# DeltaNet and a PReLU feed-forward on one core: outputs accumulated in PSUM and turned on VectorE instead of TensorE

## The chip, the core and the metric

One core of a Trainium2 chip runs the whole program. The metric is the device time of one execution in microseconds (us). Five engines work side by side, each through its own queue in order: TensorE (PE, with its weight loads as PEld), VectorE (DVE), ScalarE (ACT), GpSimd (POOL) and SyncE (SP, which issues nearly all DMAs). Work between engines is ordered by semaphores.

## What is computed

A delta-rule attention is followed by a feed-forward layer; the attention's output, with heads laid side by side, is the feed-forward's input.

```python
# q, k, v: (4 batches, 8 heads, 768, 48); beta: (4, 8, 768)
k_n = k / (norm(k) + 1e-6)
for t in range(768):
    y[t]  = q[t] @ state                     # the state before this token
    v_old = k_n[t] @ state
    state = state + beta[t] * outer(k_n[t], v[t] - v_old)
x = y as (3072 tokens, 384)
h = x @ w_in                                 # 384 x 2048
out = (max(h, 0) + alpha * min(h, 0)) @ w_out   # 2048 x 384
```

All of it is float32.

## The kernel before

**Chunks and steps.** The 768 tokens are cut into 12 chunks of 64. A step n is one chunk for two of the four batches: 24 steps, `steps[n] = (c, bp)`, so an even and the following odd step make up one chunk c (n = 2c and 2c + 1). A chunk's 256 token rows are the unit of the feed-forward.

**One step of attention.** In the order of the data: `through_state` (L799) multiplies keys with the state and with the turned queries; three VectorE subtractions (L809) make the right-hand side r and L521 masks the query-key products a_t. `solve` (L824) multiplies r with the inverse of the chunk's triangular matrix, and L828 weighs the result to u. `outputs` (L837) multiplies a_t with u, `next_state` (L853) keys with u, and L861 subtracts that from the state. `query` (L784) multiplies the queries with the state before the step; ScalarE copies the result from PSUM to y (L788), and L843 on VectorE adds the product of `outputs` to it. `to_ffn` (L876) turns y on TensorE, three 128x128 transposes against the identity into a PSUM bank, and L878 on ScalarE copies the turned block into xt, the feed-forward's input for the chunk.

**Preparing later steps.** `grams` (L501) multiplies keys with keys eight steps ahead; L507 weighs the result in two VectorE pieces, `keep` (L554) moves one block. Every four steps, `eliminate` inverts the small triangular blocks on VectorE in many short pieces (L593, L599) with 32x32-block transposes (L566). `between` (L733) builds the off-diagonal blocks, which ScalarE copies out (L745). `turn_q` (L466) turns a step's queries by one VectorE transpose, `load_q` fetches them (SP).

**The feed-forward.** `ffn_in` (L966) multiplies xt with w_in, 512 columns to a PSUM bank; L976 on ScalarE takes the negative part and L978 on VectorE adds it with its slope. `ffn_out_fast` (L1031) multiplies with w_out by seven products instead of eight; the operand sums are L920. From chunk 8 on `ffn_in_fast` (L1189 to L1237) and `ffn_out_faster` (L1283) do the same with fewer TensorE products and with more work on ScalarE, GpSimd and VectorE; L1151 makes sums of the chunk's xt beforehand.

**The order.** The order on every engine is written out by the program. From step 6 (JOINED) on, each step has two bursts of attention products on TensorE, and the feed-forward, a generator of equal parts, fills the stretches between: `burst_a` (outputs and next_state of step n - 1, through_state of step n), a filled stretch, `turn_round` (to_ffn of step n - 1, then the turn of keys, of queries n + 2, the weights and load_q n + 3), a second stretch, `burst_b` (solve n, grams n + 9, query n + 1, between), a third stretch. FILL and FILLS say how many parts each stretch takes: 12, 10, 12 in even and 12, 18, 12 in odd steps. A chunk's feed-forward has 76 parts, which is what two steps take. `weave` interleaves the pieces of other engines by their share of a stretch.

**PSUM.** From step 8 (NARROW) on there are two double banks for the attention (p_pair) and four single banks for the feed-forward (p_ffn, p_more). `ps_big` hands out the double banks in turn. Different engines reading the same bank are ordered one behind the other.

Of the kernel before, what the change touches and what calls it, by code (L numbers as in the profile page):

```python
# [25 lines left out]
FP32 = mybir.dt.float32  # L26
# [18 lines left out]
def kernel(  # L45
# [31 lines left out]
    def ps_big():  # L77

        big.append(big.pop(0))
        return big[-1]  # L80
# [24 lines left out]
    def half(i):  # L105
        return slice(64 * i, 64 * i + 64)

    def dims(i):
        return slice(64 * i, 64 * i + D)
# [375 lines left out]
    def now(pieces):  # L485
        for x in pieces:
            x()
# [7 lines left out]
    def grams(n, p=None):  # L495

        if n >= N:
            return []
        p = region(p, G * C, g=G)
        for g, a, t in quarters():  # L500
            nc.tensor.matmul(  # L501
                p[half(t), a, g], k_t[n][dims(a), g, half(t)], k_t[n][dims(a), g, half(t)]
            )

        def weighted(dst, cols):
            w = stats[n][1][:, 0:2, :, None].to_broadcast([128, 2, G, HB])
            nc.vector.tensor_tensor(  # L507
                out=dst.rearrange("p (a g) i -> p a g i", a=2), in0=p[:, :, :, cols], in1=w,
                op=ALU.mult,
            )  # L510

        return [
            lambda: weighted(gather(n), slice(0, HB)),
            lambda: weighted(right[n % EARLY][:, 1:], slice(HB, C)),
            lambda: keep(n),
        ]
# [136 lines left out]
    def quad(i):  # L653
        return slice(HB * i, HB * i + HB)
# [123 lines left out]
    def query(n, p=None):  # L778
        if n >= N:
            return []  # L780
        bp = steps[n][1]
        p = region(p, G * D, g=G)
        for g, a, t in quarters():
            nc.tensor.matmul(  # L784
                p[half(t), a, g], q_t[n][dims(a), t, g], state[bp][dims(a), t, g]
            )
        ys[n] = work.tile([128, H, D], FP32, name="y")
        return [lambda: nc.scalar.copy(by_parity(ys[n]), p)]  # L788

# [31 lines left out]
    def solve(n, p=None):  # L821
        p = region(p, G * D, g=G)
        for g, a, t in quarters():
            nc.tensor.matmul(  # L824
                p[half(t ^ a), a, g], inv[n % NE][half(t), a * G + g], rhs_[n][half(t), a, g]
            )
        us[n] = work.tile([128, 2, G, D], FP32, name="u")
        return [lambda: nc.vector.tensor_tensor(  # L828
            out=us[n], in0=p,
            in1=stats[n][1][:, 0:3:2, :, None].to_broadcast([128, 2, G, D]), op=ALU.mult,  # L830
        )]

    def outputs(n, p=None):
        c, bp = steps[n]
        p = region(p, G * D, g=G)
        for g, a, t in quarters():
            nc.tensor.matmul(  # L837
                p[half(t), a, g], a_t[n][half(t ^ a), a * G + g], us[n][half(t ^ a), a, g]
            )
        if c == 0:  # L840
            ys[n] = work.tile([128, H, D], FP32, name="y")
            return [lambda: nc.scalar.copy(by_parity(ys[n]), p)]
        return [lambda: nc.vector.tensor_tensor(  # L843
            out=by_parity(ys[n]), in0=by_parity(ys[n]), in1=p, op=ALU.add
        )]

    def next_state(n, p=None):
        c, bp = steps[n]
        pieces, wide = [], n < 2 * NJ
        if c < NCH - 1:  # L850
            p = region(p, G * D, g=G)
            for g, a, t in quarters():
                nc.tensor.matmul(  # L853
                    p[half(a) if wide else dims(a), t, g], k_late[n % NKL][half(t ^ a), 2 * g + a, 0 : C if wide else D],
                    us[n][half(t ^ a), a, g],
                )


            def less(rows):
                x = state[bp][rows]  # L860
                nc.vector.tensor_tensor(out=x, in0=x, in1=p[rows], op=ALU.subtract)  # L861

            if wide:
                pieces = [lambda: less(slice(0, 2 * C))]
            else:
                pieces = [lambda: less(dims(0)), lambda: less(dims(1))]
        return pieces

    def to_ffn(n, p=None):
        c, bp = steps[n]  # L870
# [500 lines left out]

    WY, JOINED = G * D, NJ + 2

    def burst_a(n):

        soon, later = [], []
        b = ps_big()
        if n > JOINED:
            soon += outputs(n - 1, b[:, :, 0:WY])
            soon += next_state(n - 1, b[:, :, WY : 2 * WY])  # L1380
            later.append(lambda: load_late(n + 1))
        if n < N:
            p = ps_big()
            y = ps_big()[:, :, 0:WY] if n < NARROW else None
            soon += through_state(n, p[:, :, 0 : G * (D + C)], y)
            if n < JOINED + 2:
                soon += between_1(n + 1, b[:, :, 2 * WY : 2 * WY + G * HB])
            if n == JOINED:
                soon += grams(n + EARLY, big[-1][:, :, WY : WY + G * C])
                later.append(lambda: squares(n + EARLY + 1))  # L1390
            later.append(lambda: load_v(n + 3))
        now(soon)
        return later

    def burst_b(n):

        b, x = ps_big(), ps_big()
        soon = solve(n, b[:, :, 0:WY])
        gram = grams(n + EARLY + 1, x[:, :, 0 : G * C])
        asked = query(n + 1, x[:, :, G * C : G * C + WY]) if n + 1 >= NARROW else []  # L1400
        wanted = [(n + 1, True, b[:, :, WY : WY + G * HB])]
        if n > JOINED:
            wanted.append((n + 2, False, b[:, :, 2 * WY : 2 * WY + G * HB]))
        soon += between(*wanted)
        if n >= LATE:
            now(soon[:1])
            return soon[1:] + asked
        now(soon + asked + gram[:2])
        return gram[2:] + [lambda: squares(n + EARLY + 2), lambda: load_early(n + EARLY + 3)]

    def turn_round(n):

        if n > JOINED:
            to_ffn(n - 1)
        if n == JOINED:
            flips(n + EARLY + 1, N)
            load_keys(steps[TURNED_K][0])
        later = []
        if TURNED_K <= n + EARLY + 1 < N:
            later.append(lambda: turn_k(n + EARLY + 1))  # L1420
        if n + 2 < N:
            later.append(lambda: turn_q(n + 2))
        later += weigh(n + EARLY + 1)
        return later + [lambda: load_q(n + 3)]
# [427 lines left out]
    TURNS = [(3, 3, 4), (3, 3, 4), (4, 4, 4), (0, 5, 6)]  # L1852
    FILL = {JOINED: (8, 12, 12), JOINED + 1: (10, 12, 10), JOINED + 2: (8, 10, 12)}
    FILLS = [(12, 10, 12), (12, 18, 12)]
    put_off = []
    for n in range(JOINED, N):
        if n == NARROW:
            banks(2, 2)
        fill, share = FILL.get(n, FILLS[n % 2]), PIECES_OF.get(n, TURNS[n % NJ])
        extra = [[], [], []]  # L1860
        if n == JOINED:
            place(n + 1, (0,))
            extra[1] = [(weight_sums(1, 0, 3), 3)]
            extra[2] = [(weight_sums(0, 3, 4), 1)]
        elif n == JOINED + 1:
            extra[0] = [(weight_sums(1, 3, 4), 1, 0.6), (placing(n + 1, (1, 2, 3)), PLACING)]

        later = burst_a(n)
        stretch(fill[0], blocks, share[0], later, *extra[0], *put_off)
        put_off = []  # L1870
        later = turn_round(n)
        if n == JOINED:
            extra[1].append((placing(n + 1, (1, 2, 3)), PLACING))
        stretch(fill[1], blocks, share[1], later, *extra[1], soon=0.2)
        m, ends = (n + 6) // NJ, n % NJ == 2
        if ends and n > JOINED:
            for _ in blocks:
                assert False
            place(n + 2, (0,))
        later = burst_b(n) + [lambda: scale_v(n + 1)]  # L1880
        if n == JOINED:
            stretch(fill[2], blocks, share[2], later, *extra[2])
            for _ in blocks:
                assert False
            place(n + 2, (0,))
            place(n + 3, (0,))
            blocks = eliminate(m)
        else:
            if ends:
                blocks = eliminate(m) if m < N // NJ else iter(())  # L1890
            after = [(placing(n + 2, (1, 2, 3)), PLACING)]
            if n % NJ != 1:
                after.append((placing(n + 3, (0,)), 1))
            if n >= LATE:
                put_off, after = after, []
            stretch(
                fill[2], blocks, share[2], later, *after, *extra[2], soon=0.1 if n >= LATE else 0.5
            )
# [34 lines left out]
```

## Time and profile before

| | |
|---|---|
| median of 3 runs | 647.7 us (647.32 to 648.19) |
| the profiled execution | 647.16 us |
| its span in the trace | 645.4 us |
| TensorE busy | 630.1 us (98%) |
| VectorE busy | 502.9 us (78%) |
| ScalarE busy | 253.0 us (39%) |
| GpSimd busy | 94.0 us (15%) |
| granted TensorE clock | 0.999 of full speed |

The span is the time from the first to the last instruction of the core in the trace; the execution lies 1.8 us around it. Matmuls are pipelined, so a busy TensorE may still not be at its peak; the chain of work that ended last and the waits tell whether it was held up. In the views, a line such as L876 is a line of the kernel before; tiles carry the program's names.

### The profile page before, as it was taken

Reading aid. Unit: us, or ns where it says so; the run is one execution under the profiler, and the core shown is the slowest. Engines: PE = TensorE matmul, PEld = TensorE weight load, DVE = VectorE, ACT = ScalarE, POOL = GpSimd, SP = SyncE. Lnnn points to the kernel's source line nnn. Section 1 sums busy time; section 2 is a strip of 40 time slices with the busy share of each in tenths; the row PEclk is TensorE's granted clock in tenths of the full one; section 3 lists DMA queues with packets and bytes.
Section 4 is the critical chain, followed back from the end, with each engine's and each line's share of the span. In section 5 each row is a group of like instructions: output and inputs, shape, how many; then the busy total and the mean of one; then the engine's idle time right before and its main releaser. Section 6 shows DMA issues by size and latency. Waiting matters only on the chain.

```text
span 645.4 us, 21564 instructions
## 1 busy us (share of the span) xinstructions
PE 630.1 (98%) x9199; PEld 556.2 (86%) x9199; DVE 502.9 (78%) x1206; ACT 253.0 (39%) x599; POOL 94.0 (15%) x204
## 2 busy tenths in 40 slices
PE   5999999999999999999999999999999999999997
PEld 4678888557778988988988988988999999999997
DVE  3986988977999879768979869769879569477383
ACT  5978565344453342243242243133145054041240
POOL 6001211010000000001000000000044053062360
PEclk9999999999999999999999999999999999999999
DMA  8967725211353243242242122122121220100000
GB/s 122 296 136 170 232 60 153 62 38 35 52 79 51 39 65 51 38 67 48 39 76 39 25 46 32 26 47 30 32 51 20 42 36 2 39 1 3 26 0 25
DMA packets 145968, 39.26 MB, mean 61 GB/s; under 512 B 139040, under 2 KB 142256, under 8 KB 145872
## 3 DMA queue, kind: packets, MB, share of 16 engines
q1 hardware_dynamic: 144000, 37.40, 28.4%
q8 instruction: 72, 1.18, 0.8%
q10 hardware_dynamic: 1872, 0.49, 0.4%
q14 instruction: 24, 0.20, 0.1%
HBM read 33.14 MB, written 4.72 MB: 59 GB/s over the span
## 4 chain that ended last, share of the span: by engine, by line
PE 77%; DVE 13%; ACT 5%; issue 2%; DMA 2%; SPq 1%; POOL 1%; DVEq 0%; POOLq 0%; ACTq 0%
PE p_ffn L966 12%; PE p_more L1283 8%; PE p_more L1031 7%; PE p_ffn L1031 7%; PE p_more L966 7%; PE p_ffn L1009 5%; PE p_more L1199 5%; PE p_ffn L1189 3%; PE p_ffn L1283 3%; PE p_ffn L1194 2%; DVE block L599 2%; PE p_pair L799 2%; PE p_pair L837 2%; PE p_pair L824 2%; PE p_pair L733 2%
## 5 line engine op out<-in xcount | busy, mean ns | idle before, releaser
L966 PE MATMUL p_ffn<-xt,w_in 128*128 128x256 f32 x528 | 123.1, 384 | 1.8 <-DVE act L978 1.8
L966 PEld LDWEIGHTS p_ffn<-xt,w_in 128*128 128x128 f32 x528 | 97.5, 190 | 16.0 <-ACT wgt L718 1.6
L966 PE MATMUL p_more<-xt,w_in 128*128 128x256 f32 x240 | 54.8, 381 | 0.0
L599 DVE TENSOR_TENSOR block<-block,prod 128x30 f32<-128x30 f32 (+9 forms) x150 | 49.8, 332 | 5.2
L1223 POOL TENSOR_TENSOR k_t<-k_t 128x128 f32<-128x128 f32 (+1 forms) x48 | 29.6, 616 | 163.7 <-ACT k_t L1218 161.2
L878 ACT COPY xt<-p_pair 128x384 f32<-128x384 f32 x22 | 10.4, 479 | 107.5 <-PE p_pair L876 107.3
L966 PEld LDWEIGHTS p_more<-xt,w_in 128*128 128x128 f32 x240 | 45.0, 190 | 6.3
L593 DVE TENSOR_TENSOR prod<-block 128x30 f32<-128x30 f32 (+9 forms) x150 | 48.8, 325 | 1.5
L418 POOL TENSOR_TENSOR beta_t<-beta_t,rec 128x8 f32<-128x8 f32 x24 | 5.9, 245 | 280.0 <-DVE rec L412 270.4
L976 ACT ACTIVATE act<-p_ffn 128x512 f32<-128x512 f32 x36 | 21.4, 593 | 53.1 <-PE p_ffn L966 53.0
L978 DVE SCALAR_TENSOR_TENSOR act<-act,al_t,p_ffn 128x256 f32<-128x256 f32 x72 | 30.9, 471 | 8.7 <-ACT act L976 8.6
L1223 POOL TENSOR_TENSOR block<-block 128x128 f32<-128x128 f32 (+1 forms) x48 | 28.0, 583 | 15.8 <-ACT block L1218 13.3
L1189 PE MATMUL p_ffn<-xt,w_in 128*128 128x256 f32 x96 | 28.7, 380 | 0.0
L1031 PE MATMUL p_ffn<-w_out,act 128*128 128x192 f32 x160 | 27.9, 330 | 0.0
L507 DVE TENSOR_TENSOR same<-p_pair,wgt 128x256 f32<-128x256 f32 x24 | 10.1, 422 | 22.3 <-ACT y L788 17.0
L745 ACT COPY inv<-p_pair 32x256 f32<-32x256 f32 x40 | 14.5, 362 | 33.1 <-DVE u L828 32.3
L976 ACT ACTIVATE act<-p_more 128x512 f32<-128x512 f32 x20 | 11.9, 595 | 37.2 <-PE p_more L966 37.2
L1031 PEld LDWEIGHTS p_ffn<-w_out,act 128*128 128x128 f32 x160 | 25.9, 190 | 0.4
L809 DVE TENSOR_TENSOR r<-v_raw,p_pair 64x192 f32<-64x192 f32 (+1 forms) x66 | 23.3, 352 | 2.3 <-PE p_pair L799 1.2
L828 DVE TENSOR_TENSOR u<-p_pair,wgt 128x384 f32<-128x384 f32 x24 | 13.2, 554 | 14.4 <-PE p_pair L733 13.6
L1031 PE MATMUL p_more<-w_out,act 128*128 128x192 f32 x128 | 22.2, 328 | 0.0
L1009 PE MATMUL p_ffn<-w_out,act 128*128 128x384 f32 x64 | 21.7, 490 | 0.2 <-ACT w_out L262 0.2
(252 smaller groups left out, 1489.5 us busy)
## 6 DMA issues: line engine op xcount, KB each, us to landing
w_out<-in_moe_w_in_dram SPq DMA_DIRECT2D x10, 512.0 KB, 5.6
v_raw<-in_v_dram SPq DMA_DIRECT2D x48, 96.0 KB, 2.8
kl<-in_k_dram SPq DMA_DIRECT2D x96, 48.0 KB, 2.5
out_dram<-o_sb SPq DMA_DIRECT2D x90, 48.0 KB, 1.6
space_out<-in_moe_w_out_dram SPq DMA_DIRECT2D x11, 384.0 KB, 4.3
ke_last<-in_k_dram SPq DMA_DIRECT2D x25, 96.0 KB, 3.1
qp<-in_q_dram SPq DMA_DIRECT2D x64, 32.0 KB, 2.2
w_out<-in_moe_w_out_dram SPq DMA_DIRECT2D x5, 384.0 KB, 4.5
```

Of the source, the lines that this page charges most:

```text
L593: nc.vector.tensor_tensor(out=prod, in0=r[:, 0:j, j : j + 1].to_broadcast([128, j, n]), in1=r[:, j : j + 1, j + 1 : HB].to_broadcast([128, ...
L599: nc.vector.tensor_tensor(out=r[:, 0:j, j + 1 : HB], in0=r[:, 0:j, j + 1 : HB], in1=prod, op=ALU.add)
L809: nc.vector.tensor_tensor(out=r[to, a], in0=v_in[to, a], in1=p[own, a, :, 0:D], op=ALU.subtract)
L966: nc.tensor.matmul(p_h[:, i], w_in[:, t, (f + i) * 128 : (f + i + 1) * 128], xt[:, t], start=(t == 0), stop=(t == KT - 1),)
L976: nc.scalar.activation(g, p_h, ACT.Relu, scale=-1.0)
L978: nc.vector.scalar_tensor_tensor(out=g[:, i], in0=g[:, i], scalar=al_t[:, f + i : f + i + 1], in1=p_h[:, i], op0=ALU.mult, op1=ALU.add,)
L1009: nc.tensor.matmul(p_o[u], gs[f // 2][:, f % 2, u * 128 : (u + 1) * 128], w_out[:, f], start=(f == 0), stop=(f == FT - 1),)
L1031: nc.tensor.matmul(p, x(i), w(i), start=(i == 0), stop=(i == FP - 1))
L1189: nc.tensor.matmul(p[:, f * 256 : f * 256 + 256], w(2, f), xt[:, 2], start=True, stop=False)
L1199: nc.tensor.matmul(q[:, j], a, b, start=True, stop=True)
L1223: nc.gpsimd.tensor_tensor(out=dst, in0=a, in1=b, op=ALU.add)
L1283: nc.tensor.matmul(p, x(i), w(i), start=(i == 0), stop=(i == FP - 1))
```

## The change

From step 8 on, y is no longer put together on VectorE. The query product and the outputs product of a step go into the same PSUM region: `query` starts the accumulation and `outputs`, half a step later, adds to it. For this the query of step n moves from `burst_b` of step n - 1 to `burst_b` of step n, ahead of the solve, and its bank (`asked_in`) is kept for `burst_a` of step n + 1. ScalarE then copies the finished sum to y, where it copied the query product before.

The turn of y for steps 8 to 22 moves off TensorE. `turn_y` is one VectorE transpose of 32x32 blocks, issued in the burst right behind the state's subtraction. `rows_y` is sixteen ScalarE copies of 32 partitions by 96 elements that put the blocks into xt. In odd steps (the first half of a chunk) eight of them go to the second and eight to the third stretch; in even steps (the second half, which completes the chunk) all sixteen go to the first stretch, from 0.4 of it on. Step 23 keeps `to_ffn`.

`turn_q` of step n + 2 moves from `turn_round` to behind `burst_b`. The second stretch of steps 9 and 11 takes 16 parts instead of 18.

```diff
@@ query
                 p[half(t), a, g], q_t[n][dims(a), t, g], state[bp][dims(a), t, g],
+                start=(n < NARROW or g == 0), stop=(n < NARROW),
             )
+        if n >= NARROW:
+            return []
@@ outputs
-        if c == 0:
+                start=(n < NARROW), stop=(n < NARROW or g == G - 1),
+        if c == 0 or n >= NARROW:
             ys[n] = work.tile([128, H, D], FP32, name="y")
             return [lambda: nc.scalar.copy(by_parity(ys[n]), p)]
+    def turn_y(n):
+        z = work.tile([128, 2, G, D], FP32, name="z", tag="r")
+        z = z.rearrange("p a g d -> p (a g d)").rearrange("p (k r i) -> p r k i", r=4, i=HB)
+        blocks_y[n] = z
+        y = ys[n].rearrange("p h d -> p (h d)")
+        nc.vector.transpose(
+            z.rearrange("p r k i -> p k r i"), y.rearrange("p (k r i) -> p k r i", r=4, i=HB)
+        )
+    def rows_y(n):
+        c, bp = steps[n]
+        if bp == 0:
+            xts[c] = work.tile([128, KT, TOK], FP32, name="xt", tag="xt", bufs=NXT)
+        z = blocks_y.pop(n)
+        to = xts[c].rearrange("p k (u b t i) -> p u b t k i", u=2, b=NB, t=2)
+        for i in range(16):
+            t, u, r = i // 8, i // 4 % 2, i % 4
+            nc.scalar.copy(to[quad(r), u, bp, t], z[quad(2 * t + u), r])
+            if i == 15 and bp == NB - 1:
+                whole.add(c)
+            yield
+    def is_turned(n):
+        return NARROW <= n < N - 1
@@ burst_a
-        b = ps_big()
+        if n > NARROW:
+            b = asked_in.pop()
+            y, z = b[:, :, G * C : G * C + WY], b[:, :, 0:WY]
+        else:
+            b = ps_big()
+            y, z = b[:, :, 0:WY], b[:, :, WY : 2 * WY]
         if n > JOINED:
-            soon += outputs(n - 1, b[:, :, 0:WY])
-            soon += next_state(n - 1, b[:, :, WY : 2 * WY])
+            soon += outputs(n - 1, y)
+            soon += next_state(n - 1, z)
+            if is_turned(n - 1):
+                soon.append(lambda: turn_y(n - 1))
@@ burst_b
+        gram = grams(n + EARLY + 1, x[:, :, 0 : G * C])
+        if n >= NARROW:
+            asked_in.append(x)
+            query(n, x[:, :, G * C : G * C + WY])
         soon = solve(n, b[:, :, 0:WY])
-        gram = grams(n + EARLY + 1, x[:, :, 0 : G * C])
-        asked = query(n + 1, x[:, :, G * C : G * C + WY]) if n + 1 >= NARROW else []
@@ turn_round
-        if n > JOINED:
+        if n > JOINED and not is_turned(n - 1):
             to_ffn(n - 1)
-        if n + 2 < N:
+        if n < NARROW:
             later.append(lambda: turn_q(n + 2))
@@ the loop over the steps
+    FILL[9] = FILL[11] = (12, 16, 12)
         later = burst_a(n)
+        if is_turned(n - 1):
+            if n % 2:
+                rows = rows_y(n - 1)
+                extra[1].append((part(rows, 8), 8))
+                extra[2].append((part(rows, 8), 8))
+            else:
+                extra[0].append((rows_y(n - 1), 16, 0.4))
         later = burst_b(n) + [lambda: scale_v(n + 1)]
+        if NARROW <= n < N - 2:
+            later.append(lambda: turn_q(n + 2))
```

More of the change, by code (lines that the diff above doesn't have):

```diff
@@ L784, in query @@
             nc.tensor.matmul(
-                p[half(t), a, g], q_t[n][dims(a), t, g], state[bp][dims(a), t, g]
-            )
+                p[half(t), a, g], q_t[n][dims(a), t, g], state[bp][dims(a), t, g],
+                start=(n < NARROW or g == 0), stop=(n < NARROW),
+            )
+        if n >= NARROW:
+            return []
         ys[n] = work.tile([128, H, D], FP32, name="y")
@@ L837, in outputs @@
             nc.tensor.matmul(
-                p[half(t), a, g], a_t[n][half(t ^ a), a * G + g], us[n][half(t ^ a), a, g]
+                p[half(t), a, g], a_t[n][half(t ^ a), a * G + g], us[n][half(t ^ a), a, g],
+                start=(n < NARROW), stop=(n < NARROW or g == G - 1),
             )
-        if c == 0:
+        if c == 0 or n >= NARROW:
             ys[n] = work.tile([128, H, D], FP32, name="y")
@@ L867, in next_state @@
         return pieces
+    blocks_y = {}
+    def turn_y(n):
[18 more added lines that the diff above has]
+            yield
     def to_ffn(n, p=None):
@@ L1372 @@
     WY, JOINED = G * D, NJ + 2
+    asked_in = []
+    def is_turned(n):
+        return NARROW <= n < N - 1
     def burst_a(n):
         soon, later = [], []
-        b = ps_big()
+        if n > NARROW:
[4 more added lines that the diff above has]
+            y, z = b[:, :, 0:WY], b[:, :, WY : 2 * WY]
         if n > JOINED:
-            soon += outputs(n - 1, b[:, :, 0:WY])
-            soon += next_state(n - 1, b[:, :, WY : 2 * WY])
+            soon += outputs(n - 1, y)
+            soon += next_state(n - 1, z)
+            if is_turned(n - 1):
+                soon.append(lambda: turn_y(n - 1))
             later.append(lambda: load_late(n + 1))
@@ L1406, in burst_b @@
             now(soon[:1])
-            return soon[1:] + asked
-        now(soon + asked + gram[:2])
+            return soon[1:]
+        now(soon + gram[:2])
         return gram[2:] + [lambda: squares(n + EARLY + 2), lambda: load_early(n + EARLY + 3)]
     def turn_round(n):
-        if n > JOINED:
+        if n > JOINED and not is_turned(n - 1):
             to_ffn(n - 1)
```

## The prediction

> **What bounds the kernel now.** I read the page's busy rows and slices first.
>
> ```profile
> PE 630.1 (98%) x9199; PEld 556.2 (86%) x9199; DVE 502.9 (78%) x1206; ACT 253.0 (39%) x599; POOL 94.0 (15%) x204
> ...
> PE   5999999999999999999999999999999999999997
> ...
> DVE  3986988977999879768979869769879569477383
> ACT  5978565344453342243242243133145054041240
> ```
>
> TensorE is at nine tenths nearly everywhere, VectorE is near it in some slices, ScalarE has room. Since a busy TensorE may still be held up, I went to the chain of work that ended last, in order of time, around 262 us.
>
> ```profile
> 261.77 0.70 DVE sums L920
> 262.48 0.04 issue
> 262.52 1.57 PE p_more L1031 x8
> 264.09 0.61 PE p_pair L837 x32
> 264.70 0.36 PE p_pair L853 x32
> 265.06 0.78 PE p_pair L799 x32
> 265.84 2.80 PE p_more L1031 x16
> 268.64 5.20 PE p_ffn L1031 x32
> 273.84 0.33 PE p_pair L876 x3
> ```
>
> Columns: start, length, engine and tile. Up to 262 us the chain runs through VectorE; from 262.52 on it is TensorE instruction after instruction to the end, with no wait between. TensorE's own waits agree: after 205 us they hold one entry, 0.4 us at 262.5 (L1031 for DVE L920). So whatever leaves TensorE after 262 us leaves the time, as long as the other engines follow. Whether they can is read from the busy time by stage (columns: window, its length, then busy us of PE, PEld, DVE, ACT, POOL):
>
> ```profile
> 409.60:432.00 22.40, 22.40 (x335) 20.65 (x331) 15.09 (x38) 4.41 (x10) 0.00 (x0) 1.00 0.24 45
> 432.00:457.00 25.00, 25.00 (x344) 22.66 (x339) 22.96 (x58) 8.19 (x21) 0.00 (x0) 1.00 0.16 26
> ```
>
> The first is an even step, the second an odd one: odd steps leave VectorE only 2.0 us free. The clock is 1.00 in both, so no throttle enters the sum.
>
> **Part by part.**
>
> *Transposes off TensorE.* Steps 8 to 22 lose their three L876 transposes. In the chain each triple is 0.33 us (273.84, 294.10, ... 576.55, fourteen of them after 262 us), and the next matmul starts right behind it: 14 x 0.33 = 4.6 us on the path. The fifteenth (244.93) lies before 262 us, where VectorE leads. Gone too are fifteen ScalarE xt copies (L878, 0.479) and sixteen VectorE adds (L843, 0.547).
>
> *One copy for another.* Steps 8 to 23 copied the query result out on ScalarE (L788, 0.479); now the accumulated output is copied, same shape and engine. Accumulating in PSUM adds no matmul: the same sixteen plus sixteen are issued. Cost 0.
>
> *The VectorE transpose, 128x384.* Bounds: L466's 128x512 at 0.705, scaled by 384/512, gives 0.53; L566's 128x256 from strided blocks at 0.652, scaled by 1.5, gives 0.98. The source here is read in order and only the destination is in blocks, as in L466, so I take 0.55. Against the add that goes (0.547) VectorE gains or loses nothing; the upper bound is +0.43 a step. [...]
>
> *Sixteen ScalarE copies a step, 32 partitions x 96 elements.* SBUF copies in this trace: 0.192 for 4 elements (L718), 0.295 for 128 (L662), 0.403 for 256 (L554). A line through them gives 0.27 at 96 (between 0.19 and 0.30), 16 x 0.27 = 4.3 us a step, +3.8 net of the xt copy, 57 us over fifteen steps: ScalarE goes from 253 to some 310 us. In time it fits (8.2 of 25.0 and 4.4 of 22.4 above). In order: in odd steps the instruction order of the changed kernel puts at most three copies ahead of a Relu (L976), 0.8 us; the Relu's engine sat idle about 2 us before each one inside a feed-forward stretch (13 waits on p_more banks, 30.1 us), which hides it. The first copy waits for the VectorE transpose, and a Relu queued behind it waits too; the copies begin 0.4 into the filled stretch or after it, 2 us and more behind the burst, when the transpose is due. In even steps all sixteen stand together, but no Relu lies between them and the next burst. Cost 0; if that cover is gone, see the first rival. The rows must be there when the next chunk starts: in step 10 the subtraction (L861) ends at 268.5, plus 0.55 and 4.3 is 273.4, and the chunk's first L966 is at 276.8 and later after the change, because two parts move. Cost 0.
>
> *Query ahead of solve.* In the second burst the Gram products (0.48 us, to step 14) and the query (0.45) now precede the solve, so u (L828) is up to 0.93 us later. In step 10 u ends at 282.2 and its reader L837 starts at 286.96: 4.8 us of cover, 3.9 left. Cost 0. The four ScalarE copies behind u (1.5 us) still end before L799 at 287.9.
>
> *The turn of q, half a step later* (L466, 0.705, same count). Its reader is more than a step away. load_q on SP waits for the turn of the step before, which stands one filled stretch ahead: cost 0; without it the 1.55 us of the qp DMA, seen once in the chain at 248.07, would return.
>
> *VectorE's waits.* The waits show what the move of the query frees:
>
> ```profile
> DVE same L507 <- ACT y L788: 17.0, 8, 2.1
> ```
>
> That is 2.1 us in each of steps 7 to 14: the first reader of the Gram bank waited for the four ScalarE copies and the y copy. In the changed order L507 waits for no ScalarE instruction. Three of them (6.4 us) lie before 262 us, where VectorE leads. In exchange the state's subtraction (L861, now behind a ScalarE copy of the same bank) waits in every burst from step 9 on: between 0 (VectorE behind anyway) and 1.1 us (a 0.6 us Relu just begun, then 0.48). Behind it on VectorE stand the transpose, L809 and L521, and the Relu partners L978 that free feed-forward banks. Net for steps 9 and 10 VectorE gains at least 1 us, so I count the 0.4 us wait at 262.5 and the fifteenth triple (0.33) as gained; bounds 0 and 0.73. [...]
>
> *Fills of steps 9 and 11.* Two parts fewer each; the same products run behind the last step. Cost 0.
>
> **Sum.** 4.62 + 0.33 + 0.40 = 5.35 us off the profiled execution's 647.16 (span 645.4 and 1.8 around it): 641.8. That execution stands 0.54 under the median 647.7, so the forecast for the median is 642.4.
>
> **Rivals.**
> 1. *A copy in front of a Relu shows.* One 0.27 us copy delays a bank in each of the eight odd steps: 2.2 us back, 644.6. For it: Relus and copies alternate there. Against it: four banks of 2.6 us each and 2.0 us of idle.
> 2. *Rows late for the chunk.* The chunk's first product waits for the sixteenth copy in the seven even steps from 10 on; at 0.7 us each 4.9 us return, 647.3: no change. It needs the rows 3.4 us later than reckoned. The same time would come out if the transposes were not on the path after all (TensorE's ends are modelled).
> 3. *VectorE becomes the bound in odd steps: slower.* A transpose at its upper bound (+0.43) and a 0.6 us wait for ScalarE make 1.03 us. If VectorE's 2.0 us of slack are not free where they are needed, just behind the burst, eight odd steps hand 1.03 us each to TensorE: +8.2, 650.6. It decides from 0.67 us a step upward (5.35 over eight). For it: 22.96 of 25.0 busy. Against it: L507's wait goes in steps 8 to 14, and in step 17 VectorE had caught up at the burst (it waited for L853 at 457.18).
>
> **Numbers.** Forecast 0.66 (its own range 641.0 to 643.5), rival 1 0.15, rival 2 0.08, rival 3 0.11. About 0.2% (1.3 us) is what a measurement can tell from no change, so the forecast and rival 1 count as faster (0.81), rival 2 as the same (0.08), rival 3 as slower (0.11). The range runs from 640.3 (the forecast with 2 us more from weight-load waits that vanish with the bursts' new order: TensorE's loader lists 4.5 us "issue" before L837 in all) to 646.4, which takes in rival 1 and leaves out the other two.
>
> **What would show it.** In the profile after: TensorE some 5 us less busy, L876 at 21 instead of 66 transposes into p_pair, bursts following each other 0.33 us sooner; no TensorE wait above 0.5 us after 262; the L507 wait gone, a new one of the state's subtraction for the y copy below 1.1 us; 240 copies near 0.27; ScalarE near 310. I am wrong if TensorE shows repeated waits for DVE act L978 or for xt, or if VectorE's odd windows reach 25 of 25.

## The result and the profile after

The changed kernel takes 651.92 us (median of 13 runs, 650.21 to 653.82) beside 647.7 (646.05 to 651.14) of the kernel before: a ratio of 1.0067, interval 1.0055 to 1.008. It is slower, where 642.4 was forecast. The profiled execution took 652.41, with a span of 650.7 and a clock of 1.0.

In the changed kernel the lines stand lower: `ffn_in` is L996 (L966 before), its Relu L1006 and VectorE partner L1008, the sums L950, `ffn_out_fast` L1061 (L1031), u L831, the y copy L846, the turn L881, the row copies L894; L704, L707 and L745 keep their numbers. The page of the changed kernel, the rows that were shown of before:

```profile
PE 629.2 (97%) x9154; PEld 552.3 (85%) x9154; DVE 498.2 (77%) x1205; ACT 313.1 (48%) x824; POOL 93.3 (14%) x204
...
PE   6999999999999998999999999999999999999997
...
DVE  4976998967999888858978857968967668567383
ACT  5887565345453344635544634435447356354140
```

TensorE is no longer full: the slice from 244 to 260 us falls to 8. VectorE has less to do, not more, and ScalarE is only half busy. No engine became the bound by its work. TensorE's waits behind 203 us (engine, line, what it waited for; us in all, times, longest), where before had one of 0.4 us:

```profile
PE p_ffn L1061 <- DVE act L1008: 3.1, 2, 2.3
PE p_more L1061 <- DVE act L1008: 2.8, 2, 1.5
PE p_more L1229 <- ACT block L1248: 1.2, 2, 0.6
PE p_ffn L996 <- issue: 0.4, 1, 0.4
PE p_more L1313 <- DVE act L1267: 0.4, 2, 0.2
```

The first two rows are four waits, at 260.72 (2.25 us), 309.91 (1.25), 359.39 (1.53) and 407.68 (0.82): one behind the second burst of each of the steps 9, 11, 13 and 15. The stages shown of before, even and odd:

```profile
409.60:432.00 22.40, 22.40 (x333) 21.14 (x333) 16.86 (x45) 7.11 (x24) 0.00 (x0) 1.00 0.25 46
432.00:457.00 25.00, 25.00 (x331) 22.24 (x330) 22.28 (x56) 12.22 (x34) 0.00 (x0) 1.00 0.16 25
```

In these two windows, behind step 15, TensorE is full again, and VectorE's odd window has 22.28 of 25.0, not 25. The small waits for L1248 and L1267 lie later, in steps 19 and 21.

Since start-up differs from one execution to the next, edit or not (the stretch told here begins at 200.0 us in e10 and at 204.2 in the same kernel's e12), I compare the kernels below by one stretch: from the first product behind a wait that all of them have near 202 us to the end of TensorE's last product, split into work and the waits listed by the trace. Before: 440.44 = 440.04 work + 0.40 idle. After: 444.85 = 436.99 + 7.86. So 3.05 us of work did go, and 7.46 us of waiting came.

**Where the wait comes from.** Three engines in step 11 of the changed kernel, TensorE first, then VectorE, then ScalarE (start, length, engine, line, tiles, count, and in brackets the idle time before and what ended it):

```profile
301.20 1.03 PE L996 MATMUL p_more<-xt,w_in 128*128 128x256 f32 x4
...
304.39 1.99 PE L996 MATMUL p_more<-xt,w_in 128*128 128x256 f32 x8
306.22 2.44 PE L1061 MATMUL p_more<-w_out,act 128*128 128x192 f32 x14
309.91 0.59 PE L1061 MATMUL p_more<-w_out,act 128*128 128x192 f32 x2 [1.25 <-DVE act L1008]
```

```profile
305.00 0.55 DVE L831 TENSOR_TENSOR u<-p_pair,wgt 128x384 f32<-128x384 f32 x1
...
309.38 0.87 DVE L1008 SCALAR_TENSOR_TENSOR act<-act,al_t,p_more 128x256 f32<-128x256 f32 x2 [2.57 <-ACT act L1006]
```

```profile
302.03 0.27 ACT L894 COPY xt<-z 32x96 f32<-32x96 f32 x1
305.58 0.73 ACT L745 COPY inv<-p_pair 32x256 f32<-32x256 f32 x2 [3.29 <-DVE u L831]
306.33 0.74 ACT L745 COPY mid<-p_pair 32x256 f32<-32x256 f32 x2
307.08 0.51 ACT L704 ACTIVATE inv<-inverse,which 128x256 f32<-128x256 f32 x1
307.50 0.39 ACT L707 COPY diag<-turned 128x256 f32<-128x256 f32 x1
307.89 0.83 ACT L894 COPY xt<-z 32x96 f32<-32x96 f32 x3
308.75 0.60 ACT L1006 ACTIVATE act<-p_more 128x512 f32<-128x512 f32 x1
```

Read from the bottom. The last bank of the chunk's `ffn_in` is cut by the burst: four products ahead of it, eight behind it, done at 306.4. Its Relu begins at 308.75, more than 2 us later. The four copies L745 stand ahead of it in ScalarE's queue and wait for u, which VectorE ends at 305.55. From then on ScalarE works without a gap: the four copies, L704, L707 and three row copies, 3.17 us together, then the Relu; behind it come VectorE's partner and then the output products. In before this bank ended at 302.2, ahead of the burst, and its Relu stood ahead of the copies; the burst hid it (TensorE, then ScalarE, in step 11 of before):

```profile
299.44 2.75 PE L966 MATMUL p_more<-xt,w_in 128*128 128x256 f32 x12
```

```profile
302.23 0.60 ACT L976 ACTIVATE act<-p_more 128x512 f32<-128x512 f32 x1 [1.99 <-PE p_more L966]
305.06 0.74 ACT L745 COPY inv<-p_pair 32x256 f32<-32x256 f32 x2 [2.23 <-DVE u L828]
```

Nothing here is an added operation but 0.83 us of row copies: an order has flipped. The two parts fewer in step 9, and two more in step 11, moved the feed-forward late against the bursts. The page has it in one group, first of before, then of after (the last field is idle time ahead of the copies):

```profile
L745 ACT COPY inv<-p_pair 32x256 f32<-32x256 f32 x40 | 14.5, 362 | 33.1 <-DVE u L828 32.3
```

```profile
L745 ACT COPY inv<-p_pair 32x256 f32<-32x256 f32 x40 | 14.5, 362 | 84.7 <-DVE u L831 83.9
```

The same forty copies have 51.6 us more of idle time ahead of them. That says that the order on ScalarE has changed, but not where it costs. Step by step, 47.4 of the 51.6 us lie in the even steps 10 to 22 and only 2.6 in the steps 9, 11, 13 and 15. In step 10 the idle time goes from 1.94 to 8.16 us, and there too a Relu that stood ahead of the copies now runs behind them, but no TensorE wait follows.

### The profile page after: what moved, and what is told of

The parts are those of the page before. It is cut to its first block, busy times and chain, and to the rows that moved or that the text cites. A ratio compares the mean times of both kernels' runs of the same rounds, so it can differ in the third digit from the quotient of the medians.

```text
span 650.7 us, 21683 instructions
## 1 busy us (share of the span) xinstructions
PE 629.2 (97%) x9154; PEld 552.3 (85%) x9154; DVE 498.2 (77%) x1205; ACT 313.1 (48%) x824; POOL 93.3 (14%) x204
## 4 chain that ended last, share of the span: by engine, by line
PE 71%; DVE 13%; ACT 5%; SPq 4%; DMA 3%; issue 2%; POOL 1%; ACTq 0%; DVEq 0%; POOLq 0%
PE p_ffn L1061 9%; PE p_ffn L996 8%; PE p_more L1061 7%; PE p_more L1313 7%; PE p_ffn L1039 6%; PE p_more L1229 4%; PE p_more L996 4%; PE p_ffn L1313 3%; PE p_ffn L1219 3%; DVE act L1008 3%; PE p_ffn L1224 2%; SPq L153 2%; PE p_pair L733 2%; PE p_pair L1480 2%; PE p_pair L802 2%
## 5 line engine op out<-in xcount | busy, mean ns | idle before, releaser
L996 PE MATMUL p_ffn<-xt,w_in 128*128 128x256 f32 x528 | 124.1, 384 | 2.4 <-DVE act L1008 1.8
L996 PEld LDWEIGHTS p_ffn<-xt,w_in 128*128 128x128 f32 x528 | 97.4, 190 | 17.5 <-ACT wgt L718 1.6
L894 ACT COPY xt<-z 32x96 f32<-32x96 f32 x240 | 64.4, 268 | 25.7 <-DVE z L881 22.6
L996 PE MATMUL p_more<-xt,w_in 128*128 128x256 f32 x240 | 55.7, 382 | 0.0
L745 ACT COPY inv<-p_pair 32x256 f32<-32x256 f32 x40 | 14.5, 362 | 84.7 <-DVE u L831 83.9
L996 PEld LDWEIGHTS p_more<-xt,w_in 128*128 128x128 f32 x240 | 44.9, 190 | 6.3
L1008 DVE SCALAR_TENSOR_TENSOR act<-act,al_t,p_ffn 128x256 f32<-128x256 f32 x72 | 31.2, 475 | 17.6 <-ACT act L1006 17.6
L1006 ACT ACTIVATE act<-p_ffn 128x512 f32<-128x512 f32 x36 | 21.4, 595 | 36.7 <-PE p_ffn L996 36.6
L1061 PE MATMUL p_ffn<-w_out,act 128*128 128x192 f32 x160 | 28.1, 329 | 3.1 <-DVE act L1008 3.1
L1061 PEld LDWEIGHTS p_ffn<-w_out,act 128*128 128x128 f32 x160 | 26.2, 190 | 4.1 <-DVE act L1008 3.7
L1219 PE MATMUL p_ffn<-xt,w_in 128*128 128x256 f32 x96 | 29.3, 387 | 0.0
L831 DVE TENSOR_TENSOR u<-p_pair,wgt 128x384 f32<-128x384 f32 x24 | 13.2, 553 | 18.0 <-PE p_pair L733 17.1
L1008 DVE SCALAR_TENSOR_TENSOR act<-act,al_t,p_more 128x256 f32<-128x256 f32 x40 | 17.3, 472 | 11.7 <-ACT act L1006 11.7
L1061 PE MATMUL p_more<-w_out,act 128*128 128x192 f32 x128 | 22.5, 328 | 2.8 <-DVE act L1008 2.8
L1061 PEld LDWEIGHTS p_more<-w_out,act 128*128 128x128 f32 x128 | 20.9, 190 | 3.5 <-DVE act L1008 3.4
L554 ACT COPY same<-right 32x256 f32<-32x256 f32 x29 | 11.7, 403 | 22.7 <-DVE right L507 19.1
```

What stands on the lines that cost most here:

```text
L894: nc.scalar.copy(to[quad(r), u, bp, t], z[quad(2 * t + u), r])
L996: nc.tensor.matmul(p_h[:, i], w_in[:, t, (f + i) * 128 : (f + i + 1) * 128], xt[:, t], start=(t == 0), stop=(t == KT - 1),)
L1008: nc.vector.scalar_tensor_tensor(out=g[:, i], in0=g[:, i], scalar=al_t[:, f + i : f + i + 1], in1=p_h[:, i], op0=ALU.mult, op1=ALU.add,)
L1061: nc.tensor.matmul(p, x(i), w(i), start=(i == 0), stop=(i == FP - 1))
L1219: nc.tensor.matmul(p[:, f * 256 : f * 256 + 256], w(2, f), xt[:, 2], start=True, stop=False)
```

## The experiments

Theory A: the shorter fills push the Relu of a chunk's last bank behind the four copies that wait for u. Rival B: the row copies delay the Relu wherever it is. Rival C: VectorE is the bound in odd steps (the prediction's third rival).

In the last column, the stretch is the one from the wait near 202 us to TensorE's last product, in us.

| kernel | ratio to before, interval | median us | stretch = work + idle |
|---|---|---|---|
| before | 1 | 647.7 | 440.44 = 440.04 + 0.40 |
| after | 1.0067, 1.0055 to 1.008 | 651.92 | 444.85 = 436.99 + 7.86 |
| e1, old fills | 0.991, 0.9893 to 0.9926 | 641.58 | 435.29 = 434.90 + 0.39 |
| e2, fills alone | 1.013, 1.0109 to 1.0152 | 655.51 | 448.11 = 443.00 + 5.11 |
| e3, rows early | 1.0013, 0.9996 to 1.0029 | 648.31 | 441.17 = 436.43 + 4.74 |
| e4, sum alone | 1.0061, 1.004 to 1.0082 | 650.88 | 443.64 = 440.26 + 3.38 |
| e5, e4 shifted | 1.007, 1.0057 to 1.0084 | 652.87 | 443.34 = 441.19 + 2.15 |
| e6, longer fill | 0.9954, 0.994 to 0.9967 | 645.23 | 438.27 = 435.88 + 2.39 |
| e7, one part | 1.0102, 1.0084 to 1.0119 | 654.42 | 446.66 = 438.20 + 8.46 |
| e8, copies late | 0.9952, 0.9939 to 0.9966 | 645.27 | 438.00 = 436.05 + 1.95 |
| e9, late and given back | 0.9939, 0.9921 to 0.9957 | 643.15 | 435.39 = 435.02 + 0.37 |
| e10, late, old fills | 0.994, 0.9922 to 0.9959 | 643.01 | 435.30 = 434.91 + 0.39 |
| e11, e1 again | 0.9923, 0.9909 to 0.9937 | 642.75 | 435.31 = 434.91 + 0.40 |
| e12, e10 again | 0.9918, 0.9896 to 0.994 | 642.43 | 435.31 = 434.90 + 0.41 |

e1 to e4, e5 to e8, e9 with e10 and e11 with e12 ran beside before on one chip each, where before had 647.63, 648.34, 647.35 and 647.7.

**e1, the change with the old fills.**

```diff
-    FILL[9] = FILL[11] = (12, 16, 12)
```

> The change without its fill line: steps 9 and 11 take 18 parts in the second stretch again. Theory A (the shorter fills push the last feed-forward bank of a chunk behind the second burst, so that its Relu on ScalarE stands behind the four copies that wait for u, and the first output product waits): the four waits of 0.8 to 2.3 us (5.9 us in all) at the start of the output products in steps 9, 11, 13 and 15 go, and so do the 1.2 us of waits for L1248; 643 to 645.5 us. Rival B (the row copies on ScalarE delay the Relu wherever the bank stands): the waits stay, 650 to 652 us. Rival C (VectorE is the bound in odd steps): no change beyond 1 us, 651 to 652.

Faster, by 0.9% (again 0.77% in e11); at 641.58 it is even below the range of A. TensorE's only wait behind 203 us is the 0.4 us "issue" before L996. The busy row of its page:

```profile
PE 625.2 (98%) x9154; PEld 551.6 (86%) x9154; DVE 501.8 (78%) x1205; ACT 312.3 (49%) x824; POOL 93.0 (15%) x204
```

ScalarE and VectorE do the same work as in the change, within 4 us; all the other waits are gone. ScalarE in step 11 of this kernel:

```profile
300.98 0.60 ACT L1006 ACTIVATE act<-p_more 128x512 f32<-128x512 f32 x1 [1.14 <-PE p_more L996]
303.84 0.74 ACT L745 COPY inv<-p_pair 32x256 f32<-32x256 f32 x2 [2.27 <-DVE u L831]
```

The Relu is ahead of the copies, and the copies' wait has nobody behind it that matters. The one line of the fills costs 9.56 us of the stretch (444.85 - 435.29). C falls, and B as the cause: with all row copies and all of VectorE's new work, nothing waits.

**e2, the fills alone on the kernel before.**

```diff
+    FILL[9] = FILL[11] = (12, 16, 12)
```

> The kernel before with the change's fill line alone. Theory A: the same waits for DVE act L978 at the start of the output products of steps 9, 11, 13 and 15 appear without any row copy, 5 to 6 us in all: 651 to 654 us. Rivals B and C: the same products in another place, no row copies and no new wait on VectorE: 647 to 648.5 us.

Slower by 1.3%, without one row copy, and 1.5 us above the range of A. TensorE's waits behind 203 us:

```profile
PE p_ffn L1031 <- DVE act L978: 3.3, 2, 2.9
PE p_more L1031 <- DVE act L978: 1.8, 2, 1.1
```

These are again the four waits behind the bursts of steps 9, 11, 13 and 15 (260.6, 311.59, 361.32, 409.8). The stretch grows by 7.67 us: 4.71 of waits and 2.96 of work. The fills are enough by themselves.

**e3, the change with all sixteen rows of an odd step in the second stretch.**

```diff
-                extra[1].append((part(rows, 8), 8))
-                extra[2].append((part(rows, 8), 8))
+                extra[1].append((rows, 16))
```

> The change with all sixteen row copies of odd steps in the second stretch, none behind the second burst; the fills stay short. Theory A: only the one to three row copies of 0.27 us that stood ahead of the late Relu go, its wait for u and the copies behind u stays: 649.5 to 651.5 us, the four waits shorter by 0.3 to 0.8 us each. Rival B: the waits go altogether, 644 to 646.5 us.

At 648.31 us it lies between the two expectations. With no row copies behind the copies that wait for u, the four waits shrink from 5.85 to 3.16 us (1.99, 0.45, 0.72, none in step 15), the stretch by 3.68. So the row copies are not the cause (e2 has none), but they have a part in the size: in steps 11, 13 and 15 the wait shrinks by 0.80 to 0.82 us, and the three row copies of step 11 took 0.83.

**e4, the accumulation alone: old fills, y turned by `to_ffn` as before.**

```diff
-        return NARROW <= n < N - 1
+        return False
-    FILL[9] = FILL[11] = (12, 16, 12)
```

> The accumulation in PSUM alone, with the moved query and the moved turn of q; the turn of y stays on TensorE for all steps, and the fills are those of before. Theory A: TensorE's work is that of before and the accumulation costs nothing on the path: 646.5 to 648.5 us. Rival C (VectorE held behind ScalarE's copy of the same bank): 649.5 us or more, with TensorE waits behind the bursts.

650.88, above what A expected; by the time it is C, but C's sign, waits behind the bursts, is not there. The stretch has 440.26 of work, 0.22 more than before, so accumulating and moving the query hardly adds to TensorE's work. But two waits came that no theory had, in steps 13 and 14, in the middle of the small matmuls L733 of the second burst:

```profile
353.90 0.25 PE L733 MATMUL p_pair<-diag,right 32*32 32x32 f32 x3 [1.47 <-issue]
```

"Issue" says that nothing in the trace released it. Both (1.47 and 1.49) make 2.96 of the 3.38 us of idle time; without them it would stand at about 647.9, within what A expected. That is arithmetic, not a run.

**e5, e4 with eight more small matmuls in the warm-up at the start.**

```diff
-    for _ in range(6):
+    for _ in range(14):
         busy(0.25, mid[1])
```

> The accumulation alone (fills as before, y still turned on TensorE), with eight more small warm-up matmuls at the very start, which shift everything that TensorE executes by eight instructions and change nothing else. It asks what the two stalls of 1.5 us are that the accumulation alone showed in the middle of L733 in steps 13 and 14, where no other engine released TensorE. Theory S, they hang on where the instructions lie in TensorE's stream: they move to another place or go, and the time changes by 1 us or more (647 to 652). Theory T, they belong to these bursts: they stay at the same matmuls, 650.5 to 651.5.

Both waits are gone from their places. One of 2.15 us has come, in step 8, again within L733:

```profile
236.99 0.26 PE L733 MATMUL p_pair<-diag,right 32*32 32x32 f32 x1 [2.15 <-issue]
```

The time is 0.9 us over the expected range; the stretch, 443.34, is about e4's, but begins at 204.56 instead of 201.92, as e12's does without any such edit. The waits do not stay at the same matmuls, so T falls. Of S, they do move, but the time does not: the stretch differs by 0.30 us. So e4 and e5 leave open whether the accumulation has a part in these waits. What is known of their places is told in the last section.

**e6, two parts more instead of fewer in step 9.**

```diff
-    FILL[9] = FILL[11] = (12, 16, 12)
+    FILL[9] = (12, 20, 12)
```

> The changed kernel with its fill line turned the other way: the second stretch of step 9 takes 20 parts where the kernel before has 18 and the change 16; step 11 keeps 18. Order theory (A): what costs is that the Relu of a chunk's last ffn_in bank falls behind the four copies that wait for u; with two parts more it stays ahead of them, so TensorE has no wait behind the bursts of steps 9, 11, 13 and 15, and the time is that of the change with the old fills, 641.6, give or take 1.5. Rival D, any shift of the parts off the old fills costs (the old numbers are the only good ones): waits of the same 5 to 6 us in all come back at some other place, 647 to 652.

645.23: above A's 641.6 (+-1.5), below D's 647. The waits behind the copies are away, as A has it, but one of 0.71 us in step 13 is left, where L1061 now starts ahead of the burst and needs its operands sooner than VectorE (busy without a gap there) reaches L1008, another of 0.17 us in step 18, and 1.1 us in steps 19 and 21. So of the fills that were tried the old ones are the best, with losses on both sides, and A alone does not tell the whole price of a shift.

**e7, one part fewer in step 9 only.**

```diff
-    FILL[9] = FILL[11] = (12, 16, 12)
+    FILL[9] = (12, 17, 12)
```

> The changed kernel with 17 parts in the second stretch of step 9 and 18 again in step 11: the feed-forward is shifted by one part from there on, where the change shifts it by two and then four. In the written-out order this one part already puts the Relu of the last ffn_in bank behind the four copies, in steps 9, 11, 13 and 15. Order theory (A): the cost is that of the flipped order, hardly of how far the parts move, so the four waits stay, 4 us or more together, and the time is 647 to 652. Rival P, the cost is in proportion to the parts moved: a quarter to a half of 10.3 us over 641.6, 643.5 to 646.5, with waits below 3 us together.

```profile
PE p_more L1061 <- DVE act L1008: 4.3, 2, 2.8
PE p_ffn L1061 <- DVE act L1008: 3.8, 2, 2.3
```

One part, where the change moves two and then four, costs more than these: 8.1 us of waits (2.26, 1.50, 2.77, 1.56, steps 9 to 15), 654.42, over the upper end of A's range. P falls: the price comes with the flipped order and does not grow with the distance. In step 11 TensorE reaches the output products sooner than in the change (at 305.58, the change at 306.22), while the Relu stands in the same queue behind u (at 308.35, the change at 308.75); so the wait is longer with the smaller shift, 1.50 against 1.25 us. That is read from one step, not tested.

**e8, the change with its short fills, but the four copies of steps 9, 11, 13 and 15 issued behind the burst.**

```diff
+        if n in (9, 11, 13, 15):
+            now(soon[:1] + gram[:2])
+            return soon[1:] + gram[2:] + [
+                lambda: squares(n + EARLY + 2), lambda: load_early(n + EARLY + 3)
+            ]
```

> The changed kernel with its own short fills; in steps 9, 11, 13 and 15 alone the four copies L745 that wait for u are issued later, among the first pieces of the stretch behind the burst, so that the Relu of the last ffn_in bank stands ahead of them on ScalarE. Order theory (A): the waits of 0.8 to 2.3 us behind these four bursts go (below 0.5 each); the small waits of steps 20 and 22 on (1.2 to 2 us in all) stay; 643 to 647. Rival E, the Relu is late for another reason (its bank, the row copies, VectorE): the waits stay and the time is 650 to 653.

ScalarE in step 11 now (this kernel runs 2.9 us ahead of the change here):

```profile
301.76 0.83 ACT L894 COPY xt<-z 32x96 f32<-32x96 f32 x3
303.51 0.60 ACT L1006 ACTIVATE act<-p_more 128x512 f32<-128x512 f32 x1 [0.93 <-PE p_more L996]
304.14 0.51 ACT L704 ACTIVATE inv<-inverse,which 128x256 f32<-128x256 f32 x1
304.66 0.55 ACT L894 COPY xt<-z 32x96 f32<-32x96 f32 x2
305.11 0.73 ACT L745 COPY inv<-p_pair 32x256 f32<-32x256 f32 x2
```

The Relu waits for nothing but its own bank, and all four TensorE waits are gone, at unchanged fills, unchanged row copies and an unchanged cut of the bank. The stretch loses 6.85 us against the change. Only the order was changed, so this shows A directly. The idle time ahead of L745 is still 72.7 us here.

**e9, e8 with the four parts given back in steps 13 and 15.**

```diff
+    FILL[13] = FILL[15] = (12, 20, 12)
```

> The kernel of the late copies, with the four parts that steps 9 and 11 lost given back in steps 13 and 15 (20 parts in their second stretch), so that from step 16 on the feed-forward lies against the bursts as with the old fills. With the late copies alone 1.95 us of small TensorE waits were left in steps 20 to 23 (L1229 for ScalarE's L1248, L1313 for VectorE). Theory A with a second place, the shift costs a second time in the last chunks: these waits go and the time is 1 to 3.5 us under that of the late copies alone (ratio to before 0.990 to 0.9935, 641.5 to 644). Rival F, what is left has nothing to do with the shift (the late copies themselves cost): ratio 0.994 to 0.997.

The stretch is 435.39, e1's within 0.1 us, and the last small waits (L1229, L1313; by the trace they lie in steps 19 and 21, where the expectation has 20 to 23) are gone. The 2.61 us that this takes off e8's stretch are 1.58 of waits and 1.03 of work. By the stretch it is A; the ratio of 0.9939 lies between the two expectations.

**e10, e8 with the old fills.**

```diff
-    FILL[9] = FILL[11] = (12, 16, 12)
```

> The change with the old fills, and the four copies L745 of steps 9, 11, 13 and 15 issued behind the burst as in the run of the late copies. With the old fills the Relu stands ahead of these copies anyway, so theory A expects nothing of the move: ratio to before 0.990 to 0.9925, as with the old fills alone (0.991). Rival F, issuing the copies later costs by itself (the next burst waits for what they deliver): 0.9935 or more.

Its ratio of 0.994 falls to F, its stretch of 435.30 and its want of any wait to A. The two contradicted each other, so both kernels ran once more, side by side.

**e11 and e12, e1 and e10 unchanged, side by side on one chip.**

> The change with the old fills once more, beside the same kernel with the late copies, in one call. Their profiled stretches on TensorE, from the wait near 202 us to its last product, were equal (435.3 us each) while their ratios to before, taken in different calls, were 0.991 and 0.994. Theory A (the late copies cost nothing): the two ratios agree within 0.0015 here. Rival F (they cost by themselves): this one is at 0.991 and the other 0.0025 or more above it.

> The change with the old fills and the late copies, beside the same without the late copies. Theory A: the two ratios agree within 0.0015, and the stretch on TensorE is 435.3 us again. Rival F: this one is 0.0025 or more above the other.

0.9923 and 0.9918, and the same 435.31 in both: equal. The late copies cost nothing that can be seen, and the 0.003 between e1 and e10 did not come back. The change with the old fills, 0.991 and 0.9923 of before, beats both kernels; nothing tried clearly beats it.

## Why the prediction was wrong

**The step that failed** is "Fills of steps 9 and 11. Two parts fewer each; the same products run behind the last step. Cost 0." It counted the products and not their place. e1 and e2 price it: 9.56 us of the stretch on the change, 7.67 alone. Of the 9.56, the order on ScalarE in steps 9 to 15 holds 6.85 (e8): 5.85 of waits and 1.0 of work. The rest, 2.61, is the part of the shift that e9 gives back in steps 13 and 15: 1.58 of waits in steps 19 and 21 and 1.03 of work. That work grows with the waits is seen in one place: in step 11 of the change the wait splits sixteen output products into 2.44 + 0.59 us, in e8 they take 2.76 in one piece. These ends are modelled, so it is a sign and not a sum.

**The step beside it** looked at the right queue with the wrong question. "The four ScalarE copies behind u (1.5 us) still end before L799": they do, for their own readers. Who stands behind them on ScalarE was not asked, and the Relus were searched only for row copies ahead of them ("at most three copies", 0.8 us: measured 0.83). In step 11 of the change the Relu's bank was complete at 306.4, and ScalarE still went through the copies, L704, L707 and the row copies ahead of it until 308.75.

**The rest of the sum held, by its total.** With the fills as they were, the stretch fell by 5.15 us where 5.35 was reckoned, and the ratios of 0.991 and 0.9923 on the median of 647.7 are 641.9 and 642.7 beside 642.4.

- Transposes off TensorE: fifteen of the 17 triples of L876 in the stretch are gone in e1; at 0.33 us from the start of a triple to the next product that is 4.9 us (reckoned 4.62 + 0.33). The wait of 0.40 at 262.5 went, but one of 0.39 at 234.4 came, so of this term nothing was left.
- The VectorE transpose: 0.578 (taken 0.55). It is longer than the 0.33 us of the three transposes in TensorE's chain of before; still, in e1, with the move and the old fills, the stretch is 5.15 us shorter.
- Row copies: 240 at 268 ns (taken 0.27); ScalarE 313.1 us (taken 310).
- VectorE's waits: L507 for the y copy is gone. The new waits for the y copy L846 come to 2.2 us (state subtraction, 2 times, longest 1.1) and 1.7 (transpose, once) behind 203 us; the upper bound of 1.1 for the subtraction was met, but not in every burst, and the wait of the transpose was not reckoned.
- Accumulation and query ahead of the solve: the number of matmuls changed by the 45 transposes alone (9199 to 9154; the trace lists 32 and 32 of query and outputs a step, where the prediction says sixteen), and e4 has 0.22 us more work. Cost 0 held for the work. Whether the waits of 2.96 us in e4 belong to it stays open; in e1, which accumulates too, they are absent.

**The rivals.** Rival 1 (a copy in front of a Relu) named the place where it happened but the wrong copies, and priced it at 2.2 us. Rival 2 did not happen: no TensorE wait for xt. Rival 3 came nearest in time (650.6) and was wrong in cause: VectorE got less busy, and in e1 does the same work without a wait. The sign that the prediction set against itself, repeated waits for VectorE's partner of the Relu, is the one that came.

## What to carry to other kernels

When a schedule written by hand is shifted by a part, go through every in-order queue and look which pairs of neighbours have changed places, above all across an instruction that waits for another engine; count the wait of the one in front, and the work behind it, as a delay of the one behind (in step 11 of the change ScalarE's 3.29 us of idle time and 3.17 of work). Here it cost where the delayed result was needed at once, behind the second bursts of the odd steps 9 to 15, and not in the even steps. Idle time ahead of an unchanged group of instructions (33.1 to 84.7 us) hints at a changed order, but is no measure of the price: it is 72.7 us in e8, where the four waits are gone, and 56.0 in e7, where they come to the most. The waits of the engine that is the bound tell most of the price (7.47 of the 9.56 us between e1 and the change). A price with a threshold can't be scaled from the size of the edit: one part cost more than four (a stretch of 446.66 us in e7, 444.85 in the change).

## What the runs showed of the hardware

TensorE's "issue" waits gather at a few counts of its stream. Counted in recorded matmuls from the start of the trace (a few records may be missing), those of 0.1 us and more in the twelve profiles of before, after and e1 to e10 all fall near one of six counts: 726, 854, 1490, 3650, 5435 and 5818. Near 3650, e1 and eight others have 0.37 to 0.43 us among the large matmuls L996. In e5 eight matmuls were added ahead, which the trace records as sixteen (9215 instead of 9199); it waits at the same count 3650, which there lies within the small ones of L733, and waits 2.15. e4 has 5435 and 5818 within L733, and waits 1.47 and 1.49.

The count alone does not decide. In before and in e2 all three counts, 3650, 5435 and 5818, lie within L733 as well, and in e5 the last two do, and none of these has a wait.

The distances from one count to the next are 128, 636, 2160, 1785 and 383. What makes TensorE wait at these counts was not shown: the trace names no releaser. e4 has as many matmuls as before (9199) and two such waits of 2.96 us together; why it has them stays open. An experiment on a few microseconds is therefore best read with its list of waits, and not by its time alone.
